# GateLoop attention and a PReLU MLP in one kernel: v's 16-token rows from the input, phases turned by ScalarE, new due times

## The chip, the cores and the metric

The kernel runs on one core of a Trainium2 chip. Time is device time in microseconds (us), lower is better. The engines are TensorE (PE, matmuls; PEld is its weight load), VectorE (DVE), ScalarE (ACT), GpSimd (POOL) and SyncE (SP), which here issues every DMA.

## The reference

Two stages. The first is a linear attention with a complex decay per channel, for 4 batches, 8 heads, 768 tokens and head dimension 48; the second a two-layer MLP on 3072 rows of 384, with 2048 hidden features and a PReLU.

```python
mag = np.sqrt(a_re * a_re + a_im * a_im)
scale = np.minimum(mag, 0.999) / (mag + 1e-06)
a_re_n, a_im_n = (a_re * scale, a_im * scale)
for t in range(S):
    ar, ai = (a_re_n[:, :, t, :, None], a_im_n[:, :, t, :, None])
    new_re = ar * S_re - ai * S_im
    new_im = ar * S_im + ai * S_re
    kv = np.einsum('bhd,bhe->bhde', k[:, :, t], v[:, :, t])
    S_re, S_im = (new_re + kv, new_im)
    y[:, :, t] = np.einsum('bhd,bhde->bhe', q[:, :, t], S_re)
x = y.transpose(0, 2, 1, 3).reshape(B * S, H * D)
h = x @ w_in
g = np.maximum(h, 0.0) + alpha * np.minimum(h, 0.0)
out = g @ w_out
```

## The kernel before

**Units and gates.** Tokens are cut into chunks of 128; a unit is one chunk of one batch, 24 in all. The token loop is replaced by products: a decay is split into a magnitude and a phase (a unit complex number). `gates` runs nine times, each time over one to three chunks of one batch (384, 768 or 1152 values in each of 128 partitions). It computes the magnitudes' products over dyadic blocks (`dec`, stored to the scratch `decs`) and the running product of the phases over tokens (stored to `phs`). Each unit then multiplies q and k with the phases (L678), forms masked products of q and k in blocks of 1, 2, 4, 8, 16 and 32 tokens by `meet` and `mask_out` (L688, L705, L708), where W is ScalarE's copy of one half of k (L753), multiplies these with v's rows (L820), adds what the carried state gives (L827) and stores its result to `ysc` (L847). `loads_x` reads it back as xT (L860), the input of the MLP: `features` (L871, then L879 on ScalarE and L881 on DVE), `outputs` (L891, then L899 and the store L902).

**Phases' layout.** In `gates` the running product over a row of N values is made in L = 8 steps. The values are held as (l n), l outside, so that each step is one contiguous piece; L331 turns them into this order. At the end every block is multiplied with the product of the blocks before it (L440, DVE, 2N values) and the two products are added (L442, DVE, N values). In the kernel before, L442 writes into `ab` in the order of tokens, (n l), a stride of 8 values, and L444 stores `ab` from there to `phs`:

```python
TT(out=p.rearrange("p (n l) -> p l n", l=L), in0=m[:, 0], in1=m[:, 1], op=ALU.add)
used = yield DMA(N / 2, ts)
```

`tmp` has four rows of N: c, d, e and f. d and e are also UT, the operand of both multiplications at L440; c and f hold m, the products.

**v's rows.** For each block size h the product needs v's rows of the even or odd blocks of h tokens, in the tile VL (7 kinds of 2 x 64 partitions). `loads_v` fetches them per unit. For 1, 2, 32 and "odd" they are loaded from the input in pieces at L658: 1 + 1 + 2 + 2 pieces for each of two halves, 12 in all. For the sizes in SPREAD = [4, 8, 16], `half_rows` first copies the rows from the input to a scratch `vsc` in DRAM (L595: 4 DMAs for each size and batch, and for the first chunk alone), and L661 reads the three kinds at once.

**Weights.** w_in and w_out come as pairs of 32-bit words in eight pieces each (L507), through a ring of three buffers in `g_sb`, and are made into f32 by `to_f32` on ScalarE, DVE and TensorE (L520 to L548).

**The order of work.** A planner, `Plan`, writes the order of instructions of each engine ahead of time. Each generator yields its next step with its engine, an estimated cost and what it waits for. Among the steps that can start within 0.1 us of the earliest the planner takes the one that is due first. Due times are written by hand in GATES_DUE, UNIT_DUE and UNIT_STEPS and in the calls of `plan.add` (first, last and number of steps). A cost only shapes the order; the chip then runs each engine's queue in that order and waits where it must. A step of SP is one DMA issue, counted as 0.45 us; `DVE(N)` is 0.17 + 0.00105 N us, `ACT(N)` 0.17 + 0.00085 N us.

Of the kernel before, what the change touches and what calls it, by code (L numbers as in the profile page):

```python
# [11 lines left out]
ALU = mybir.AluOpType  # L12
# [3 lines left out]
P = 128  # L16
# [115 lines left out]
def kernel(  # L132
# [92 lines left out]
    def DVE(n, *after, takes=(), first=False):  # L225
        return "DVE", 0.17 + n * 1.05e-3, after, takes, 0, first

    def ACT(n, *after, takes=(), first=False):
        return "ACT", 0.17 + n * 0.85e-3, after, takes, 0, first
# [7 lines left out]
    def DMA(kb, *after, takes=(), engine="SP"):  # L237
        return engine, 0.45, after, takes, kb, False
# [20 lines left out]
    def gates(b, c0, c1):  # L259
# [57 lines left out]
        L = 8  # L317
# [117 lines left out]


        m = tmp[:, 0::3].rearrange("p a (l n) -> p a l n", l=L)
        for o, p in enumerate((x, y)):
            yield DVE(2 * N, t)
            TT(out=m, in0=UT, in1=turned(off3, o).unsqueeze(2).to_broadcast([P, 2, L, nb]), op=ALU.mult)  # L440
            ts = yield DVE(N)
            TT(out=p.rearrange("p (n l) -> p l n", l=L), in0=m[:, 0], in1=m[:, 1], op=ALU.add)  # L442
            used = yield DMA(N / 2, ts)
            nc.sync.dma_start(phs[o].rearrange("(t p) s -> p t s", p=P), p.rearrange("p (t s) -> p t s", t=NK))  # L444
        t = used
        for u in range(b * NCH + c0, b * NCH + c1):
            done["PP", u] = t
        done["gates", b + last, 0 if last else c1] = used
# [122 lines left out]


    KINDS = ["odd"] + LEVELS
    SPREAD = [4, 8, 16]
    vsc_of = {}

    def half_rows():


        for b, chunks in [(0, 1)] + [(b, NCH) for b in range(B)]:  # L580
            vsc = dram.tile([len(SPREAD), chunks, 2, HC, 2 * D2], F32, tag=f"vsc{chunks}", name="vsc")
            for c in range(1 if (b, chunks) == (0, NCH) else 0, chunks):
                vsc_of[b * NCH + c] = vsc[:, c]
            for i, h in enumerate(SPREAD):
                for n in range(HP):
                    src = v[b, n].rearrange("(m s h) c e -> s m h c e", s=2, h=h)[0]
                    dst = vsc[i, :, n // 2, :, (n % 2) * D2:(n % 2 + 1) * D2].rearrange(
                        "c (m h) e -> m h c e", m=src.shape[0])
                    if chunks == 1:
                        dst, src = dst[:, :, 0], src[:, :, 0]  # L590

                    k = (HP * i + n) * NCH // (HP * len(SPREAD))
                    end = yield DMA(24.5 * chunks, ("KQ", (b - 1) * NCH + k) if b else
                                    ("raw", "in", k // 3 if chunks == 1 else k))
                    nc.sync.dma_start(dst, src)  # L595
            for c in range(1 if (b, chunks) == (0, NCH) else 0, chunks):
                done["halves", b * NCH + c] = end
# [3 lines left out]
    def loads():  # L601
        for u in range(NU):
            b, c = divmod(u, NCH)
            cols = slice(c * P, (c + 1) * P)
            yield DMA(196, takes=(R["KQ"],))
            KQ = work.tile([D2, 2, H, P], F32, tag="KQ", name="KQ", bufs=3)
            for i in range(2):
                rows = slice(i * D, (i + 1) * D)
                if i:
                    yield DMA(196)  # L610
                nc.sync.dma_start(KQ[rows, 0], qv[b, :, :, cols])
                t = yield DMA(196)
                nc.sync.dma_start(KQ[rows, 1], kv_in[b, :, :, cols])
            done["KQ", u] = t
            loaded[u] = L = dict(KQ=KQ)
            for i in range(2):
                rows = slice(i * D, (i + 1) * D)
                t = yield DMA(196, ("PP", u), takes=() if i else (R["PP"],))
                scr, phs, at = scr_of[u]
                if i == 0:  # L620
                    L["PP"] = PP = work.tile([D2, H, P], F32, tag="PP", name="PP", bufs=1)
                nc.sync.dma_start(PP[rows], phs[i].rearrange("(h d) s -> d h s", d=D)[:, :, at * P:(at + 1) * P])
            done["rotation", u] = t
            for i in range(2):
                rows = slice(i * D, (i + 1) * D)
                t = yield DMA(393, ("T", u), takes=() if i else (R["T"],))
                if i == 0:
                    L["T"] = T = work.tile([D2, H, TL], F32, tag="T", name="T", bufs=2)
                nc.sync.dma_start(T[rows], scr.rearrange("(h d) c s -> d h c s", d=D)[:, :, at])
            done["decays", u] = t  # L630

    def loads_v():
        for u in range(NU):
            b, c = divmod(u, NCH)
            yield DMA(196, ("KQ", u), takes=(R["V"],))
            L = loaded[u]
            L["V"] = V = work.tile([P, HP, D2], F32, tag="V", name="V", bufs=2)
            nc.sync.dma_start(V, v[b, :, :, c].rearrange("n p e -> p n e"))
            yield DMA(98)
            VL = work.tile([P, len(KINDS), 2, D2], F32, tag="VL", name="VL", bufs=2)  # L640
            first = True
            for k, h in enumerate(KINDS):
                for i in range(2):
                    tokens = v[b, 2 * i:2 * i + 2, :, c].rearrange("n t e -> t n e")
                    to = VL[HC * i:HC * (i + 1), k]
                    if h in ("odd", 1):
                        runs = [(to, tokens[int(h == "odd")::2])]
                    elif h == 2:
                        runs = [(to[j::2], tokens[j::4]) for j in range(2)]
                    elif h == 32:  # L650
                        runs = [(to[h * m:h * (m + 1)], tokens[2 * h * m:2 * h * m + h]) for m in range(2)]
                    else:
                        runs = []
                    for dst, src in runs:
                        if not first:
                            yield DMA(98 // len(runs))
                        first = False
                        nc.sync.dma_start(dst, src)  # L658
            t = yield DMA(98 * len(SPREAD), ("halves", u))
            k = KINDS.index(SPREAD[0])  # L660
            nc.sync.dma_start(VL[:, k:k + len(SPREAD)].rearrange("p l n e -> p l (n e)"),  # L661
                              vsc_of.pop(u).rearrange("l i t e -> (i t) l e"))
            L["Vp"] = {name: VL[:, i] for i, name in enumerate(KINDS)}
            done["V", u] = t
# [261 lines left out]
    for name in ("own", 2, 4, 8):  # L926
# [2 lines left out]
    done["gates", 0, 0] = (0.0, None)  # L929

    GATES_DUE = [
        (26.3, -358.9), (-328.0, -500.0), (-179.2, -104.7), (231.5, 215.9), (74.2, 238.4),
        (540.5, 303.2), (421.2, 501.6), (664.0, 601.5), (562.3, 925.7)]
    UNIT_DUE = [
        (55.8, 57.9), (20.4, 80.3), (107.9, 169.0), (50.5, 95.0), (275.8, 246.6), (335.9, 313.3),
        (43.9, 199.5), (280.3, 275.6), (311.8, 314.1), (175.3, 359.9), (286.9, 484.9), (523.3, 614.1),
        (483.1, 533.3), (602.0, 688.0), (422.4, 760.9), (498.5, 590.6), (482.1, 685.9), (628.1, 681.9),
        (514.5, 511.7), (850.0, 972.4), (718.0, 832.2), (573.9, 747.6), (1029.2, 947.3), (1075.1, 1018.2)]
    UNIT_STEPS = [
        1.37, 1.44, -1.25, 0.34, 0.06, 0.73, -0.28, 0.17, 0.47, 0.29, 0.10, -1.28,  # L940
        -0.19, 0.89, 0.94, 0.47, -0.37, -0.85, -1.49, -0.06, 0.35, 0.20, -0.85, 0.60,
        1.37, 0.28, -0.19, -0.34, 0.29, -0.08, 0.46, -0.39, 0.38, 0.11, -1.18, 0.44,
        -2.22, -0.49, 1.07, 1.78, 1.02, -0.40, 1.79, 1.28, 0.11, -0.25, -0.85, -1.16,
        0.63, 3.94, 0.80, 2.84, 1.07, 1.11, 1.22, -0.82, -0.14, -1.89]
    with tc.manual_schedule():
        for g, due in zip(GATES, GATES_DUE):
            plan.add(gates(*g), *due, 100)
        plan.add(loads(), 224.1, 956.4, 8 * NU)
        plan.add(half_rows(), 30.3, 1048.1, 4 * (B + 1) * len(SPREAD))
        plan.add(loads_v(), 187.8, 1238.6, 14 * NU)  # L950
        plan.add(pieces(), 49.2, -71.3, 33)
        plan.add(weights("in"), -35.2, 101.3, 11 * 8)
        plan.add(weights("out"), -3.1, 99.9, 11 * 8)
        for u in range(NU):
            plan.add(unit(u), *UNIT_DUE[u], 56, UNIT_STEPS)
        plan.add(loads_x(), -1.0, -1.0, 1)
        plan.add(all_mlp(), 925.1, 925.1, 1)
        plan.run()
# [37 lines left out]
```

## Time and profile before

| | us |
|---|---|
| median of 3 runs (981.25 to 988.17) | 986.29 |
| the profiled execution, its own time | 986.29 |
| its span, first to last instruction | 984.6 |
| TensorE busy / DVE busy / ScalarE busy | 856.2 / 725.5 / 462.9 |
| L442, 18 additions (2254 ns at 1152 values) | 36.4 |
| L331, 18 copies (2335 ns at 1152 values) | 37.5 |
| L658, 288 DMA issues, median of one | 0.598 |
| L595, 60 DMA issues, median of one | 0.676 |

The profile is one execution. Busy time is what an engine spent in instructions; a wait is put down to the instruction or transfer that ended it. Issues of DMAs are not counted as busy, but SP does them one after the other, and their start and duration stand in SP's timeline. The granted clock is TensorE's, as a share of full speed. "<-" reads "from".

### The profile page before, as it was taken

To read this page: it belongs to the slowest core of one execution; us is meant where nothing else is said; L and a number is where in the kernel's file an instruction comes from. 1 tells how busy PE (TensorE), PEld (TensorE's weight loads), DVE (VectorE), ACT (ScalarE), POOL (GpSimd) and SP (SyncE) were. 2 spreads that over 40 slices of the span, in tenths; PEclk is the share of its full clock that TensorE was granted. 3 is DMA by queue.
4 is the path that set the end of the run, shared out by engine and by line. 5 is a ranking of instruction groups with operands and counts; after the bars stand their busy time and mean duration, and the time that the engine had idled before them with its cause. 6 is when DMAs were issued, how large, how long until landed. Compare 5 with 4: busy or idle time off the path is not lost.

```text
span 984.6 us, 24031 instructions
## 1 busy us (share of the span) xinstructions
PE 856.2 (87%) x9984; PEld 625.2 (63%) x9984; DVE 725.5 (74%) x1137; ACT 462.9 (47%) x924; POOL 162.0 (16%) x326
## 2 busy tenths in 40 slices
PE   0735737899897599999899999999999999999998
PEld 0312434678675467677676767777777777777776
DVE  6898897899879478889698778779888666531112
ACT  5554854485458134745283347444754233332122
POOL 3024027000700060006002500060006000000000
PEclk9958866999999589999999999999999999999999
DMA  6955992677268354786757575756566466200000
GB/s 191 202 176 174 242 231 67 165 157 204 73 175 166 119 123 126 157 181 140 178 115 186 99 184 122 165 121 170 119 169 147 105 141 138 67 25 18 17 9 17
DMA packets 190685, 132.44 MB, mean 135 GB/s; under 512 B 67568, under 2 KB 182384, under 8 KB 190576
## 3 DMA queue, kind: packets, MB, share of 16 engines
q1 hardware_dynamic: 190576, 130.90, 55.2%
q8 instruction: 79, 1.29, 0.6%
q14 instruction: 30, 0.25, 0.1%
HBM read 102.54 MB, written 35.68 MB: 140 GB/s over the span
## 4 chain that ended last, share of the span: by engine, by line
PE 67%; DVE 12%; POOL 6%; DMA 4%; SPq 4%; ACT 4%; issue 3%; ACTq 0%; DVEq 0%; POOLq 0%
PE ps_o L891 24%; PE ps_h L871 23%; PE ps_lv L688 7%; PE ps_y L820 4%; PE ps_kv L780 3%; POOL tmp L360 3%; DVE tmp L440 2%; PE ps_lv L728 2%; PE ps_y L827 2%; POOL blk L362 2%; DVE ab L442 2%; DVE tmp L360 2%; PE ps_kt L768 2%; DMA xT<-ysc 1%; DVE tmp L362 1%
## 5 line engine op out<-in xcount | busy, mean ns | idle before, releaser
L871 PE MATMUL ps_h<-xT,w_in_sb 128*128 128x256 f32 (+1 forms) x1344 | 302.7, 357 | 11.9 <-DMA xT<-ysc 10.8
L891 PE MATMUL ps_o<-w_out_sb,g_sb 128*128 128x384 f32 x768 | 302.5, 508 | 5.2 <-DVE g_sb L881 5.1
L871 PEld LDWEIGHTS ps_h<-xT,w_in_sb 128*128 128x128 f32 x1344 | 233.4, 193 | 83.1 <-DMA xT<-ysc 9.7
L879 ACT ACTIVATE g_sb<-ps_h,al 128x256 f32<-128x256 f32 (+1 forms) x224 | 99.3, 443 | 309.4 <-PE ps_h L871 308.4
L881 DVE SCALAR_TENSOR_TENSOR g_sb<-ps_h,al_sm,g_sb 128x256 f32<-128x256 f32 (+1 forms) x224 | 98.8, 442 | 166.9 <-ACT g_sb L879 165.5
L747 DVE TENSOR_TENSOR KQ<-KQ,T 96x512 f32<-96x512 f32 x240 | 167.7, 708 | 50.7 <-PE ps_lv L688 34.5
L891 PEld LDWEIGHTS ps_o<-w_out_sb,g_sb 128*128 128x128 f32 x768 | 133.6, 192 | 58.9 <-DVE g_sb L881 7.8
L688 PE MATMUL ps_lv<-KQ,W 96*64 96x64 f32 x1920 | 84.8, 233 | 36.8 <-ACT W L753 15.1
L688 PEld LDWEIGHTS ps_lv<-KQ,W 96*64 96x64 f32 x1920 | 69.5, 143 | 69.6 <-ACT W L753 35.8
L340 POOL TENSOR_TENSOR decays_sb<-decays_sb 128x72 f32<-128x72 f32 (+5 forms) x24 | 10.8, 448 | 443.5 <-DVE decays_sb L340 442.3
L753 ACT COPY W<-KQ 96x512 f32<-96x512 f32 x120 | 74.4, 624 | 18.0 <-DVE KQ L747 17.5
L678 DVE TENSOR_TENSOR KQ<-KQ,PP 96x2048 f32<-96x2048 f32 x24 | 55.0, 2292 | 3.5 <-DMA PP<-phs 2.7
L360 POOL TENSOR_TENSOR tmp<-blk 128x72 f32<-128x72 f32 (+1 forms) x56 | 33.7, 602 | 124.6 <-ACT blk L391 120.8
L545 PE MATMUL ps_w<-w_in_sb,ident 128*128 128x512 f32 (+1 forms) x32 | 19.7, 707 | 37.0 <-DVE run L402 24.4
L705 ACT ACTIVATE A<-ps_lv,rows 128x64 f32<-128x64 f32 x144 | 37.5, 330 | 17.1 <-PE ps_lv L688 16.5
L360 DVE TENSOR_TENSOR tmp<-tmp 128x576 f32<-128x576 f32 (+2 forms) x63 | 43.4, 690 | 1.8
L820 PE MATMUL ps_y<-A,VL 64*48 64x64 f32 x2304 | 44.2, 219 | 0.0
L546 PE MATMUL ps_w<-g_sb,ident 128*128 128x384 f32 (+2 forms) x64 | 36.0, 651 | 7.9 <-DVE g_sb L538 7.9
L780 PEld LDWEIGHTS ps_kv<-V,KT 64*96 64x96 f32 x704 | 35.8, 167 | 9.7 <-issue 5.7
L440 DVE TENSOR_TENSOR tmp<-tmp,off 128x2304 f32<-128x2304 f32 (+2 forms) x18 | 41.1, 2285 | 1.1 <-ACT off L434 0.8
L842 ACT COPY yT<-ps_y 48x256 f32<-48x256 f32 x96 | 30.8, 366 | 20.4 <-PE ps_y L827 18.6
L820 PEld LDWEIGHTS ps_y<-A,VL 64*48 64x48 f32 x2304 | 38.3, 122 | 2.6 <-issue 2.4
(115 smaller groups left out, 1051.6 us busy)
## 6 DMA issues: line engine op xcount, KB each, us to landing
T<-decs SPq DMA_DIRECT2D x48, 384.0 KB
KQ<-in_q_dram SPq DMA_DIRECT2D x48, 192.0 KB
KQ<-in_k_dram SPq DMA_DIRECT2D x48, 192.0 KB
PP<-phs SPq DMA_DIRECT2D x48, 192.0 KB
decs<-decays_sb SPq DMA_DIRECT2D x7, 1152.0 KB
phs<-ab SPq DMA_DIRECT2D x14, 576.0 KB
vsc<-in_v_dram SPq DMA_DIRECT2D x48, 144.0 KB
VL<-vsc SPq DMA_DIRECT2D x24, 288.0 KB
```

The source lines that it names most:

```text
L360: on(4 * k).tensor_tensor(out=m, in0=w[:, 1::-1].unsqueeze(2).to_broadcast([P, 2, 2, k]), in1=pairs_of(u), op=ALU.mult)
L440: TT(out=m, in0=UT, in1=turned(off3, o).unsqueeze(2).to_broadcast([P, 2, L, nb]), op=ALU.mult)
L678: nc.vector.tensor_tensor(out=KQ, in0=KQ, in1=PP.unsqueeze(1).to_broadcast([D2, 2, H, P]), op=ALU.mult)
L688: nc.tensor.matmul(t[64 * i:64 * i + 64, p], lhsT=weights(4 * i + p), rhs=moving(KQ[:, 0, 4 * i + p]), start=True, stop=True)
L747: nc.vector.tensor_tensor(out=x, in0=x, in1=decays(h)[:, i].unsqueeze(3).to_broadcast([D2, H, n, h]), op=ALU.mult)
L753: nc.scalar.copy(W.rearrange("p n t -> p (n t)").rearrange("p (m h) -> p m h", h=h), halves(KQ[:, 1].rearrange("p n t -> p (n t)"), h)[:, ...
L780: nc.tensor.matmul(kv[s][:, n], lhsT=KT[rows, n], rhs=V[rows, n // 2, (n % 2) * D:(n % 2 + 1) * D], start=True, stop=True)
L820: nc.tensor.matmul(o, lhsT=vp[64 * i:64 * i + 64, s, e_ * D:(e_ + 1) * D], rhs=a[:, HC * own:HC * (own + 1)], start=(name == "own" and not ...
L871: nc.tensor.matmul(p, lhsT=w_in_sb[:, f // 2, kk, f % 2 * P:(f % 2 + 1) * P], rhs=x_of[m][:, kk], start=(kk == 0), stop=(kk == NK - 1))
L879: nc.scalar.activation(gt, p, AF.Relu, scale=al_1[:, f:f + 1])
L881: nc.vector.scalar_tensor_tensor(out=gt, in0=p, scalar=al_sm[:, f:f + 1], in1=gt, op0=ALU.mult, op1=ALU.add)
L891: nc.tensor.matmul(sums[0], lhsT=gt[:, c * P:(c + 1) * P], rhs=w_out_sb[:, f], start=(f == 0), stop=(f == NF - 1))
```

## The change

Three things. In `gates` the last additions write in the order (l n) without stride, and ScalarE copies each of the two results into the order of tokens, from x to d and from y to e, after both additions; the stores read d and e. The next call's wait for `ab` (`used`) is then on the second copy and no longer on the second store. In SPREAD the size 16 is left out: v's rows of 16-token blocks are loaded at L658 in four pieces for each half, 20 pieces a unit in place of 12, and the scratch holds two kinds. All due times of gates, units, their steps and the loads have other values; those of `loads_x` and of the MLP do not. The change is described as loading the first weights piece by piece as well; no line of the diff touches how weights are cut.

```diff
+        tt = []
         for o, p in enumerate((x, y)):
             yield DVE(2 * N, t)
             TT(out=m, in0=UT, in1=turned(off3, o).unsqueeze(2).to_broadcast([P, 2, L, nb]), op=ALU.mult)
-            ts = yield DVE(N)
-            TT(out=p.rearrange("p (n l) -> p l n", l=L), in0=m[:, 0], in1=m[:, 1], op=ALU.add)
-            used = yield DMA(N / 2, ts)
-            nc.sync.dma_start(phs[o].rearrange("(t p) s -> p t s", p=P), p.rearrange("p (t s) -> p t s", t=NK))
-        t = used
+            t = yield DVE(N)
+            TT(out=p.rearrange("p (l n) -> p l n", l=L), in0=m[:, 0], in1=m[:, 1], op=ALU.add)
+            tt.append(t)
+        for o, (p, r) in enumerate(((x, d), (y, e))):
+
+            t = used = yield ACT(2 * N, *tt)
+            nc.scalar.copy(r.rearrange("p (n l) -> p n l", l=L), p.rearrange("p (l n) -> p n l", l=L))
+            t = yield DMA(N / 2, t)
+            nc.sync.dma_start(phs[o].rearrange("(t p) s -> p t s", p=P), r.rearrange("p (t s) -> p t s", t=NK))
...
-    SPREAD = [4, 8, 16]
+    SPREAD = [4, 8]
...
-                    elif h == 32:
-                        runs = [(to[h * m:h * (m + 1)], tokens[2 * h * m:2 * h * m + h]) for m in range(2)]
+                    elif h >= 16:
+                        runs = [(to[h * m:h * (m + 1)], tokens[2 * h * m:2 * h * m + h]) for m in range(HC // h)]
...
     GATES_DUE = [
-        (26.3, -358.9), (-328.0, -500.0), (-179.2, -104.7), (231.5, 215.9), (74.2, 238.4),
-        (540.5, 303.2), (421.2, 501.6), (664.0, 601.5), (562.3, 925.7)]
+        (-251.5, -234.4), (-137.4, -381.1), (-121.1, -13.5), (186.7, 183.0), (96.1, 124.0),
+        (497.4, 308.3), (486.6, 518.2), (594.7, 624.3), (594.1, 831.0)]
...
-        plan.add(loads(), 224.1, 956.4, 8 * NU)
-        plan.add(half_rows(), 30.3, 1048.1, 4 * (B + 1) * len(SPREAD))
-        plan.add(loads_v(), 187.8, 1238.6, 14 * NU)
-        plan.add(pieces(), 49.2, -71.3, 33)
-        plan.add(weights("in"), -35.2, 101.3, 11 * 8)
-        plan.add(weights("out"), -3.1, 99.9, 11 * 8)
+        plan.add(loads(), 54.1, 931.2, 8 * NU)
+        plan.add(half_rows(), 16.8, 1036.5, 4 * (B + 1) * len(SPREAD))
+        plan.add(loads_v(), 236.4, 1199.2, 22 * NU)
+        plan.add(pieces(), -52.1, -100.2, 33)
+        plan.add(weights("in"), -26.9, 98.5, 11 * 8)
+        plan.add(weights("out"), -28.0, 124.3, 11 * 8)
```

## The prediction

> **What bounds the kernel now.** I read the busy times first, then the windows by stage, then the list of waits, the chain, and the order of SP's queue around the longest wait. Busy time and slices (row PE is TensorE's busy tenths):
>
> ```profile
> PE 856.2 (87%) x9984; PEld 625.2 (63%) x9984; DVE 725.5 (74%) x1137; ACT 462.9 (47%) x924; POOL 162.0 (16%) x326
> PE   0735737899897599999899999999999999999998
> DVE  6898897899879478889698778779888666531112
> PEclk9958866999999589999999999999999999999999
> ```
>
> TensorE is full from the fifteenth slice (about 350 us) on. The windows put numbers to it (columns: PE, its weight loads, DVE, ACT, POOL busy; then granted clock, DMA share, GB/s):
>
> ```profile
> 0.00:150.00 150.00, 70.16 (x524) 38.75 (x524) 128.45 (x225) 85.61 (x134) 35.55 (x72) 0.81 0.78 203
> 150.00:350.00 200.00, 166.95 (x2307) 129.74 (x2306) 164.45 (x248) 103.52 (x212) 40.21 (x73) 0.89 0.58 140
> ```
>
> TensorE idles 150 - 70.2 = 79.8 us and 200 - 167.0 = 33.1 us in these two: 112.9 us of the 984.6 - 856.2 = 128.4 us that it idles at all. After 350 us only 15.5 us are left. The matmuls are untouched by the diff, so a change in time must come out of those 112.9 us, or make new gaps. There DVE is 84% busy ((128.5 + 164.5) / 350), ACT 54%. The waits of TensorE before 350 us that matter here:
>
> ```profile
> PE ps_w L545 <- DVE run L402: 24.4, 1, 24.4
> PE ps_lv L688 <- ACT W L753: 15.1, 10, 3.0
> PE ps_h L871 <- DMA xT<-ysc: 9.4, 1, 9.4
> ```
>
> The third is one gap, and SP's queue explains it. SP starts DMAs strictly in order; from 284.0 to 327.5 us it has no pause of 0.2 us:
>
> ```profile
> 290.88 10.70 SPq L658 DMA_DIRECT2D VL<-in_v_dram  x10
> ...
> 316.21 7.06 SPq L658 DMA_DIRECT2D VL<-in_v_dram  x9
> ...
> 325.92 0.54 SPq L860 DMA_DIRECT2D xT<-ysc  x1
> ```
>
> The MLP's input xT stands behind 22 pieces of v. TensorE ran dry at 322.6 and got it at 332.0. The two windows after it show a second price, the clock:
>
> ```profile
> 323.00:332.00 9.00, 0.03 (x1) 0.03 (x1) 2.85 (x5) 0.13 (x1) 0.00 (x0) 0.50 0.79 242
> 332.00:352.00 20.00, 17.66 (x239) 13.84 (x241) 11.50 (x18) 5.84 (x14) 4.99 (x7) 0.67 0.41 92
> ```
>
> At clock 0.67 the 20 us after the gap do about 13.4 us of full-speed work: some 6 us lost on top of 9.4.
>
> **What the Trainium skill says.** "SBUF — State Buffer", section "Door 1: The DMA port swizzle", says that a stride beyond a 16-byte line costs, so 4 fp32 are free. The trace agrees: L442 writes with a stride of 8 fp32 and takes 2254 ns; L313, with the same operation and size and no stride, 1351 ns. "DMA: Bandwidth & Descriptors", section "Anatomy of one DMA", says that a semaphore wait happens on the issuing sequencer before dispatch, not in the DMA engines; SP's "SPq L444 <- DVE ab L442: 56.6, 8, 17.7" agrees. "TensorE: Matmul & The Clock Gate", section "What's actually happening", says that idleness halves the clock; the 0.50 above agrees.
>
> **The parts.**
>
> *Last additions (L442).* Removed: strided writes. 14 x (2254 - 1351) + 2 x (1549 - 951) + 2 x (861 - 559) ns = 14.4 us of DVE; the unstrided rows for 768 and 384 elements are L323 (951) and the minimum of L313 (559). After 350 us TensorE is 98% busy beside it: worth nothing there. Before 350 us lie the calls on 384, 768 and two on 1152 elements: 2 x 0.30 + 2 x 0.60 + 4 x 0.90 = **5.4 us**. They are pieces of the chain of waits there; I take -5, bounds -5.4 and 0.
>
> *ScalarE's copies.* Added: 18, each reading with stride (8 l, n outside). Nearest row is L331, a copy that turns the same layout the other way: 2335, 1635 and 884 ns by size; below, an unstrided ACT pass (L289, 1164 ns). 14 x 2.335 + 2 x 1.635 + 2 x 0.884 = 37.7 us of ACT (half of that below), of which 14.4 before 350 us. ACT has 46% free there, so the sum is hidden; not so what queues behind a 2.3 us copy on an in-order engine: L753 (W, for the next masked product) and L879. At 311.0 and 313.7 us the L331 pair shows it: the next two products waited 2.01 and 0.67 us for W, and one 0.93 us for the product before. So 0 to 3.6 us for a pair. Two large pairs, around 175 and 275 us, fall where TensorE is nearly full: I take +2 each, **+4**, bounds 0 and +11 (the small pairs too). Later pairs: the MLP's matmuls cover them, 0.
>
> *The stores (L444).* Both copies wait for both additions, since they overwrite UT. From the first multiplication the second store was ready after 2 x 2.55 + 2 x 2.25 = 9.6 us, now after 2 x 2.55 + 2 x 1.35 + 2 x 2.34 = 12.5 us, the first after 10.1 instead of 4.8. SP waits in order for them, and x, V and KQ loads queue behind. The consumer of the phases hardly waited (L678 on PP: 2.7 us in all). Two large calls before 350 us at +2.9: 0 to +6, I take **+3**. On the other side ab is free after the copies and no longer after the landing of the stores: SP's wait "L282 <- DMA phs<-ab", 16.5 us in 6 times, goes. It overlaps other lateness; **-2**, bounds -4 and 0.
>
> *v's 16-token rows.* Per unit 8 more pieces at L658 (20 for 12), median 598 ns of SP each: 192 x 0.598 = 114.8 us. Gone: 20 of 60 scratch stores (L595, 676 ns), 13.5 us, and a third of VL<-vsc's bytes, with the same 24 issues. Net +101 us on SP. Bytes: a third of 48 x 144 KB, 12 x 24 KB and 24 x 288 KB, 4.7 MB, go; 192 x 24 KB = 4.6 MB come: nothing. Before 350 us 8 units are loaded: 64 x 0.598 - 14 x 0.676 = +29 us. Where SP has pauses this is hidden. Where it has none it delays what follows: in 284 to 327 us two units' pieces stand before xT, 16 x 0.598 = 9.6, at the 1.07 us seen there up to 17, less one scratch store of 0.7: **+9** for TensorE, bounds 0 and +16, because it already waits. Fourteen xT loads stand in this queue; two already had a wait on them, 9.4 and 1.4 us. I allow for one more late by one unit's pieces: **+5**, bounds 0 and +15 (a gap of the size above with its slow clock).
>
> *First weights piece by piece.* No changed line does this; raw weights come in 16 pieces in both. Zero, apart from the due times.
>
> *Due times.* They reorder every engine's instructions; work stays the same. In the early part loads of units come sooner (54.1 for 224.1), pieces of v later (236.4 for 187.8), gate 0 sooner. Nothing in the trace prices this. Bounds: it may remove the xT gap (-15), or shift the start of the MLP; value 0, as the terms above take the old order.
>
> **Sum:** -5 + 4 + 3 - 2 + 9 + 5 = +14 on the profiled execution's 984.6 us: 998.6, and with the 1.7 us around the span (986.29 - 984.6) **1000 us**. That execution is the median of the three.
>
> **The rivals.**
> A, chance 0.46: SP's queue, the sum above; 992 to 1010.
> B, 0.15, faster: the new order places xT's loads ahead of v's pieces. Place: the gap at 322.6 us. Price: -9.4 - 6 for gap and clock, -5 - 2 + 4 + 3 for the rest, -15.4: 971. It decides if the load leaves SP before about 316 us by the old clock (it took 6.0 us to land). For it: the later due of v's pieces. Against: 8 more of them, and each new order may make another gap.
> C, 0.15, no change: SP's pauses take all additions (it issues during only 19 of the 50 us from 150, and 44 of the 100 us from 750, by its timeline), xT stays as late as it is: -5 + 4 + 3 - 2 = 0, 986.
> D, 0.24, much slower: the early part gets later as a whole. The first xT load leaves SP at 145.8 us, after three units' V; 24 more pieces at the mean 0.73 us are 17 us, and a longer start at half clock costs 6 more: 14 + 23 = +37, 1023. For it: by its timeline SP is busy 45 of the first 50 us and 39 of those from 100 to 150. Against: TensorE did not wait for that first load.
>
> **The numbers.** One per cent, about what a measurement can tell, puts the limits at 976.4 and 996.2. Slower: all of D and 0.38 of A, 0.62. Same: 0.08 of A, C, 0.02 of B, 0.25. Faster: 0.13. Range 970 to 1028: below it half of B, above it a third of D, about 0.15 left out. It holds the summed upper bounds of the terms nearly whole.
>
> **What would show it.** L442 at 1.35 us; 18 new ACT copies at 2.3 us; 480 issues at L658; TensorE's waits on xT above the 10.8 us of now; early idle above 113 us; the late part as full as before. If early idle falls below 100 us and the waits on xT vanish, the reading of SP's queue is wrong; if copies take 1.2 us, ACT's term is.

## The result, and the profile after

The changed kernel takes 1020.27 us (median of 4 runs, 1018.67 to 1024.2) against 985.15 us (4 runs): a ratio of 1.0365, 95% interval 1.0316 to 1.0414. That is 35 us slower. The forecast was 14 us slower, 1000 us; the time lies in the range 970 to 1028, but the change is 2.5 times the forecast one.

The page after, the same rows as before (busy times, TensorE's and DVE's busy tenths, TensorE's clock):

```profile
PE 875.8 (86%) x9984; PEld 638.6 (63%) x9984; DVE 711.2 (70%) x1137; ACT 494.7 (49%) x942; POOL 159.5 (16%) x326
PE   0456746889997899998987999989998989999998
DVE  6798997797869786888668678957778666531112
PEclk9877867898999899999998899999999998999999
```

TensorE's row shows where it went: in the late part several of the 9s have turned into 8s, and one into a 7. The windows of the kernel after, in the stages of the prediction (PE, its weight loads, DVE, ACT, POOL busy; clock, DMA share, GB/s):

```profile
0.00:150.00 150.00, 70.95 (x522) 38.88 (x523) 126.16 (x228) 90.92 (x139) 36.42 (x72) 0.81 0.77 196
150.00:350.00 200.00, 171.99 (x2129) 130.24 (x2128) 159.64 (x242) 105.90 (x200) 42.14 (x83) 0.89 0.55 134
350.00:850.00 500.00, 469.13 (x5931) 348.88 (x5930) 374.06 (x561) 253.13 (x491) 80.97 (x173) 0.97 0.61 137
```

And the third window of the kernel before:

```profile
350.00:850.00 500.00, 488.03 (x6139) 360.38 (x6140) 396.03 (x585) 237.41 (x487) 86.20 (x183) 0.99 0.61 141
```

Up to 350 us TensorE idles 79.1 + 28.0 = 107 us, not more than the 113 us of before. From 350 to 850 us it idles 30.9 us where it idled 12.0, at a mean clock of 0.97 for 0.99. The whole span is 33.3 us longer: 13.7 us more idle, and 19.6 us more busy for the same matmuls, which ran slower. The clock accounts for most of that: the trace's clock records are either 1.0 or 0.5, and summed over them TensorE worked 66 us at 0.5 before and 100 us after. At full clock those 34 us more would have taken 17. The late part, where I had called edits free because TensorE is 98% busy, is where the time was lost.

### The profile page after: what moved, and what is told of

It reads as the page before. It is cut to its first block, busy times and chain, and to the rows that moved or that the text cites. A ratio compares the mean times of both kernels' runs of the same rounds, so it can differ in the third digit from the quotient of the medians.

```text
span 1017.9 us, 24317 instructions
## 1 busy us (share of the span) xinstructions
PE 875.8 (86%) x9984; PEld 638.6 (63%) x9984; DVE 711.2 (70%) x1137; ACT 494.7 (49%) x942; POOL 159.5 (16%) x326
## 4 chain that ended last, share of the span: by engine, by line
PE 56%; DVE 11%; DMA 11%; SPq 8%; POOL 5%; ACT 5%; issue 3%; DVEq 0%; ACTq 0%; POOLq 0%
PE ps_o L896 21%; PE ps_h L876 19%; PE ps_lv L693 5%; SPq L663 5%; PE ps_y L825 4%; PE ps_kv L785 2%; POOL tmp L360 2%; POOL blk L362 2%; PE ps_y L832 2%; DVE tmp L360 2%; DVE tmp L441 2%; DMA VL<-in_v_dram 1%; DMA T<-decs 1%; PE ps_lv L733 1%; DMA KQ<-in_k_dram 1%
## 5 line engine op out<-in xcount | busy, mean ns | idle before, releaser
L876 PE MATMUL ps_h<-xT,w_in_sb 128*128 128x256 f32 (+1 forms) x1344 | 307.9, 362 | 11.0 <-DMA xT<-ysc 11.0
L876 PEld LDWEIGHTS ps_h<-xT,w_in_sb 128*128 128x128 f32 x1344 | 236.0, 196 | 83.7 <-DMA xT<-ysc 12.2
L886 DVE SCALAR_TENSOR_TENSOR g_sb<-ps_h,al_sm,g_sb 128x256 f32<-128x256 f32 (+1 forms) x224 | 99.0, 443 | 181.7 <-ACT g_sb L884 180.0
L693 PE MATMUL ps_lv<-KQ,W 96*64 96x64 f32 x1920 | 86.4, 237 | 34.9 <-ACT W L758 23.4
L683 DVE TENSOR_TENSOR KQ<-KQ,PP 96x2048 f32<-96x2048 f32 x24 | 55.0, 2293 | 14.1 <-issue 6.8
L825 PE MATMUL ps_y<-A,VL 64*48 64x64 f32 x2304 | 49.0, 220 | 0.0
L825 PEld LDWEIGHTS ps_y<-A,VL 64*48 64x48 f32 x2304 | 44.3, 122 | 1.6 <-issue 1.2
L785 PEld LDWEIGHTS ps_kv<-V,KT 64*96 64x96 f32 x704 | 37.9, 176 | 10.3 <-issue 4.8
L785 PE MATMUL ps_kv<-V,KT 64*96 64x48 f32 x704 | 41.0, 262 | 2.6 <-ACT KT L777 2.3
```

The lines of the kernel that those rows point to most:

```text
L683: nc.vector.tensor_tensor(out=KQ, in0=KQ, in1=PP.unsqueeze(1).to_broadcast([D2, 2, H, P]), op=ALU.mult)
L693: nc.tensor.matmul(t[64 * i:64 * i + 64, p], lhsT=weights(4 * i + p), rhs=moving(KQ[:, 0, 4 * i + p]), start=True, stop=True)
L785: nc.tensor.matmul(kv[s][:, n], lhsT=KT[rows, n], rhs=V[rows, n // 2, (n % 2) * D:(n % 2 + 1) * D], start=True, stop=True)
L825: nc.tensor.matmul(o, lhsT=vp[64 * i:64 * i + 64, s, e_ * D:(e_ + 1) * D], rhs=a[:, HC * own:HC * (own + 1)], start=(name == "own" and not ...
L876: nc.tensor.matmul(p, lhsT=w_in_sb[:, f // 2, kk, f % 2 * P:(f % 2 + 1) * P], rhs=x_of[m][:, kk], start=(kk == 0), stop=(kk == NK - 1))
L886: nc.vector.scalar_tensor_tensor(out=gt, in0=p, scalar=al_sm[:, f:f + 1], in1=gt, op0=ALU.mult, op1=ALU.add)
```

## The experiments

Most of them hold the order: the planner counts the same steps, so all engines but SP issue the same work in the same order, and only the instructions under test differ. Then the same matmul can be found by its number in two traces, and the difference of its start shows where time is lost ("by the same matmuls" below). Ratios are to the kernel before, run in the same round, with their 95% intervals. Lines are those of each run's own kernel: L876 and L883 here are L871 of the kernel before, L733 and L740 its L728, L737 and L744 its L732, L683 and L690 its L678.

### Which of the three parts

**The due times alone**, with nothing else of the change:

```diff
-    GATES_DUE = [(26.3, -358.9), (-328.0, -500.0), ...
+    GATES_DUE = [(-251.5, -234.4), (-137.4, -381.1), ...
-        plan.add(loads(), 224.1, 956.4, 8 * NU)
+        plan.add(loads(), 54.1, 931.2, 8 * NU)
...
```

> The kernel before with nothing changed but the due times, which are those of the changed kernel. The order of work alone (theory 1): most of the 35 us come with it, 1010 us or more. v's pieces on SP (theory 2): under 995, as 12 pieces a unit are issued as before. ScalarE's copies (theory 3): under 995 as well.

Measured: 1039.5 us, ratio 1.0553 (1.0511 to 1.0595). The order alone can cost 54 us, more than the whole change.

**The reverse**, the changed kernel with the old due times:

> The changed kernel with the due times of the kernel before. Theory 1: within 10 us of 985. Theories 2 and 3: 1005 or more, since pieces and copies stay. A fourth theory, that due times only fit the very steps they were chosen for: 1005 or more here and in the run with the due times alone.

1043 us, ratio 1.0586 (1.0548 to 1.0624). In this order the kernel does not compute the reference's result, for a reason that was not traced, so its time can carry little; I rest on it only that it is no way back to 985. Each set of due times is bad with the other's steps: the fourth theory fits both runs, theory 1 only the first.

**The changed order without the copies**, additions strided:

```diff
-            TT(out=p.rearrange("p (l n) -> p l n", l=L), in0=m[:, 0], in1=m[:, 1], op=ALU.add)
+            TT(out=p.rearrange("p (n l) -> p l n", l=L), in0=m[:, 0], in1=m[:, 1], op=ALU.add)
...
-            nc.scalar.copy(r.rearrange("p (n l) -> p n l", l=L), p.rearrange("p (l n) -> p n l", l=L))
```

> The changed kernel with every engine's order held, but the last additions write in the order of tokens and ScalarE's 18 copies are not issued; the planner still counts them. Theory 3: falls by 10 us or more from 1020. Theories 1 and 2: stays within 5 us of 1020; my prediction's own terms for this part (-5 +4 +3 -2) say 0.

1035.5 us, ratio 1.0508 (1.0468 to 1.0548). Taking the copies away made it 15 us slower: ScalarE's copies are a gain in this order. Theory 3 falls, and with it my sum of 0 for this part.

**The changed order without the pieces**, 16-token rows through the scratch:

```diff
+    SCR = [4, 8, 16]
...
+                    if n % 2:
+                        copy(2, 2 * i + n // 2)
...
-                        nc.sync.dma_start(dst, src)
+                        if h != 16:
+                            nc.sync.dma_start(dst, src)
```

> The changed kernel with the order of the engines held, but v's 16-token rows go through the scratch again: the 192 pieces are not issued, 20 more scratch stores are, behind the others. Theory 2, which my prediction rests on: falls by 14 us or more from 1020. Theories 1 and 3: stays within 5 us of 1020.

992.0 us (9 runs), ratio 1.0068 (1.0033 to 1.0103). The pieces cost 28 us here.

**Both undone**, so that only the new order is left:

> The changed kernel's order with the instructions of the kernel before: no ScalarE copies, additions in the order of tokens, v's 16-token rows through the scratch. What is left against 985 is the new order alone. If the parts add up (copies gave 15, pieces took 28): 1007. If the copies' gain was only hiding part of the pieces' cost: 992.

1003.0 us, ratio 1.0153 (1.0126 to 1.0179). The four runs in the new order make a square:

```
new order, us        16-token rows by scratch   by pieces
strided additions            1003.0               1035.5
ScalarE's copies              992.0               1020.3
```

Step by step: +16 for the order (1003.0 against 986.6), -11 for the copies, +28 for the pieces. The sum of such steps is the whole difference by itself; what the square shows is that the parts hardly depend on each other. Taken in the other sequence, the pieces are +32 and the copies -15, 4 us away.

### Why the pieces cost

The start of the same matmul in the changed kernel and in after_held_v16:

```
matmul    after   held_v16   later by, us
1660      250.6      250.7     -0.1
3320      398.9      393.8      5.1
4150      466.7      455.7     11.0
5146      568.0      555.4     12.7
7138      731.1      718.8     12.3
7636      769.7      749.6     20.0
9130      893.8      871.3     22.5
```

Nothing up to 250 us, then a few places of 1 to 5 us each. One of them is between 440 and 467 us. SP's timeline of the kernel after (start, duration, issue):

```profile
438.83 0.98 SPq L627 DMA_DIRECT2D PP<-phs  x2
439.93 0.40 SPq L643 DMA_DIRECT2D V<-in_v_dram  x1
440.88 12.17 SPq L663 DMA_DIRECT2D VL<-in_v_dram  x20
453.10 1.13 SPq L666 DMA_DIRECT2D VL<-vsc  x1
454.27 0.70 SPq L600 DMA_DIRECT2D vsc<-in_v_dram  x1
455.08 0.94 SPq L634 DMA_DIRECT2D T<-decs  x2
```

The same place in after_held_v16:

```profile
432.50 8.28 SPq L670 DMA_DIRECT2D VL<-in_v_dram  x12
440.82 0.43 SPq L673 DMA_DIRECT2D VL<-vsc  x1
441.30 1.40 SPq L597 DMA_DIRECT2D vsc<-in_v_dram  x2
442.80 2.90 SPq L640 DMA_DIRECT2D T<-decs  x2
```

T, the decays of the next unit, stands behind 20 pieces instead of 12. From the first piece to T's issue it takes 14.2 us, with 12 pieces 10.3. The chain of waits of the kernel after goes on from there:

```profile
455.55 7.14 DMA T<-decs
...
462.81 0.10 DVE KQ L737
...
463.42 0.47 DVE g_sb L886
...
465.06 0.69 PE ps_lv L693 x16
```

DVE stands at L737 until T has landed, an addition of the MLP (L886) stands behind it in DVE's queue, and TensorE waits for both: 2.5 us at 465 us, none at this matmul in after_held_v16. DVE's waits at L737 in all (after_held_v16 has 6.1 us in their place):

```profile
DVE KQ L737 <- DMA T<-decs: 8.9, 3, 4.7
```

The forecast had named xT as the load that would be late. Against the kernel before, its longest wait stayed (9.4 us, then 9.0). But against the same order without the pieces it grew by 3.9 us; the kernel after, then after_held_v16:

```profile
PE ps_h L876 <- DMA xT<-ysc: 11.0, 2, 9.0
```

```profile
PE ps_h L883 <- DMA xT<-ysc: 7.1, 1, 7.1
```

So xT is late, as forecast, and T is as well. Another kind of gap is this, in TensorE's timeline of the kernel after:

```profile
733.37 1.09 PE L832 MATMUL ps_y<-KQ,St 96*48 96x64 f32 x30
736.79 0.31 PE L832 MATMUL ps_y<-KQ,St 96*48 96x64 f32 x2 [2.32 <-issue]
```

TensorE stops in the middle of 32 equal matmuls, 30 done, and waits for nothing that the profile shows. Summed over TensorE's gaps, those that end with "issue" are 14.8 us after, 6.7 us before, 7.2 us in after_held_v16. Of the 14.8, 3.1 us are waits that this word hides: at 321 and 399 us L733 starts as DVE's L683 ends, which had waited for PP and for T. At the other five stops, and at all that wait for nothing in the traces of before (four) and after_held_v16 (five), TensorE goes on 1.3 to 1.9 us after the end of a 16 KB packet of the DMA queue that the page calls "q8 instruction". That points to TensorE's instructions arriving late. No run tests that by itself.

The two traces can now be set side by side. The profiled executions differ by 24 us (1019.6 and 995.8). TensorE idles 17.5 us longer with the pieces: 3.9 us for xT, 5.0 us behind PP and T (at 321, 399 and 465 us), 5.1 us in the stops without a wait, the rest in small pieces; and it is 5.7 us longer busy. No single load is the cause.

**The pieces in the old order**, issued together behind those of size 2:

```diff
+    SCR = [4, 8]
...
+                    if h == 16:
+                        end = yield DMA(24.5 * chunks, ...)
+                        continue
...
-                        if not first:
+                        if not first and h != 16:
                             yield DMA(98 // len(runs))
```

> The kernel before with the order of all other engines held; v's 16-token rows come in 8 pieces more a unit, issued together behind those of size 2, and the scratch holds two kinds. Theory 2 (pieces cost wherever they stand): 1005 to 1015. If the 28 us were a matter of the new order: under 995. My prediction's terms for it: 999.

1010.2 us, ratio 1.0250 (1.0196 to 1.0303), 24 us more. Here the late load is mainly xT, as forecast; the busy times, the waits of this kernel and SP's timeline ahead of the gap:

```profile
PE 871.1 (86%) x9984; PEld 635.8 (63%) x9984; DVE 724.9 (72%) x1137; ACT 462.7 (46%) x924; POOL 160.0 (16%) x326
PE ps_h L878 <- DMA xT<-ysc: 23.4, 5, 15.5
```

```profile
322.49 2.02 SPq L665 DMA_DIRECT2D VL<-in_v_dram  x3
325.01 1.12 SPq L854 DMA_DIRECT2D ysc<-yT  x2
326.49 9.99 SPq L665 DMA_DIRECT2D VL<-in_v_dram  x17
...
339.03 0.64 SPq L867 DMA_DIRECT2D xT<-ysc  x1
```

From 10.8 us to 23.4 us in waits for xT, and one of 15.5 us. The gaps that end with "issue" did not grow here (5.7 us for 6.7). The waits are half of the price: of the 29.0 us that this execution's span is longer, 13.8 us are idle and 14.9 us are TensorE busy longer with the same matmuls (871.1 for 856.2). Its work at half clock went from 66 to 87 us, which makes 11 of these.

**Issues or bytes:** 192 DMAs that carry almost nothing, on top of after_held_v16:

```diff
+                        else:
+                            nc.sync.dma_start(spare[:, 4 * i + j], src[:, :, 0:1])
```

> after_held_v16 (992 us) with 192 DMAs added at the places of the pieces, each with the same 32 descriptors but one value of 4 bytes in place of a row of 384; nobody reads them. If the pieces cost by SP's issue and the length of the queue: 1010 or more. If they cost by their bytes or by the readers' waits for them: under 998.

1020.9 us, ratio 1.0375 (1.0306 to 1.0445): 29 us for 1/96 of the bytes, with no reader. So the pieces need neither their bytes nor a reader to cost that much. The places are not the same, though: by the same matmuls this run is 5 us behind after_held_v16 at 45 us, where the real pieces had cost nothing, and DVE waits 24.6 us for PP, for 8.7. That both come to 28 or 29 us is in part chance.

**Another issuer:** the 192 pieces from GpSimd.

```diff
-                        nc.sync.dma_start(dst, src)
+                        (nc.gpsimd if h == 16 else nc.sync).dma_start(dst, src)
```

> The changed kernel, but the 192 pieces of 16-token rows are issued by GpSimd at the same places of the order; SP keeps the rest. If the pieces cost because other loads stand behind them in SP's queue: 992 to 1005. If they cost by filling the DMA rings, whoever issues them: 1015 or more. GpSimd's own chain in the gates, behind which the issues may stand, can hide a gain.

1008.7 us, ratio 1.0203 (1.0152 to 1.0254), between the two answers: 12 of the 28 us are gone. TensorE's wait for xT falls from 11.0 to 5.8 us, its gaps that end with "issue" hardly (13.3 for 14.8). SP's queue alone is not shown to be the whole cost; the rest may lie in GpSimd's own queue or in the transfers, whoever issues them.

**Place or number:** all 480 issues stay, those of size 16 go back in the queue.

```diff
+                        if h == 16:
+                            behind.append((dst, src))
+                        else:
+                            nc.sync.dma_start(dst, src)
...
+            flush()
             done["decays", u] = t
```

> The changed kernel, all other engines' order held; all 480 issues stay, but the 8 pieces of a unit's 16-token rows are issued later in SP's queue: behind the next pair of T loads, at the latest ahead of the unit's products that read them; PP and xT loads pass them. If what counts is which load stands behind a piece: 1012 or less. If the number of issues counts: 1015 to 1025. If the pieces then come too late for their readers: above 1025, with TensorE's waits on L825.

1004.5 us, ratio 1.0193 (1.0174 to 1.0213): 16 us less with the same number of issues. The place of the pieces is worth more than half of their cost. But T is not what gained by it. For 21 of the 24 units the pieces were issued at their latest place, ahead of their readers, and T still stands behind all 20; this run at the place shown above:

```profile
434.64 8.37 SPq L674 DMA_DIRECT2D VL<-in_v_dram  x12
...
444.28 4.47 SPq L610 DMA_DIRECT2D VL<-in_v_dram  x8
448.86 0.88 SPq L641 DMA_DIRECT2D T<-decs  x2
```

Of the 24 pairs of T loads three have fewer pieces ahead of them than in the changed kernel, none after 316 us; of the 14 xT loads eleven have, and about half of the stores of the output. DVE's wait for T, 8.9 us in the changed kernel, did not fall:

```profile
DVE KQ L748 <- DMA T<-decs: 12.3, 5, 6.4
```

TensorE's gaps that end with "issue" fall from 14.8 to 5.3 us, its wait for xT stays (10.7 us), and its work at half clock falls from 100 to 80 us. Which of the DMAs that passed the pieces matters is not shown.

### The copies and the order, in the kernel before

**Copies in the old order**, both at the place of the second store:

```diff
+            for i, (src, r) in enumerate(((x, d), (y, e)) if o else ()):
+                nc.scalar.copy(r.rearrange("p (n l) -> p n l", l=L), src.rearrange("p (l n) -> p n l", l=L))
+                nc.sync.dma_start(phs[i].rearrange("(t p) s -> p t s", p=P), r.rearrange("p (t s) -> p t s", t=NK))
```

> The kernel before with every engine's order held, but the additions write without stride and ScalarE copies; both copies and both stores stand at the place of the second store. If this part is worth 15 us whatever the order (dropping it cost the changed kernel 15): 970 to 975. My prediction's terms for it: 985. If it only helps in the order it was planned with: 985 or more.

998.7 us, ratio 1.0125 (1.0073 to 1.0177). The same edit gains 11 to 15 us in one order and loses 12 in the other, where the planner had not counted the copies on ScalarE. By the same matmuls this run is 6 us ahead of the kernel before at 350 us and 9 us behind at the end: the gain that I had forecast for the early part is there, and the loss comes where I had put nothing. DVE's 14 us saved are no gain by themselves.

**A small disturbance** of the due times of the units:

```diff
-        (55.8, 57.9), (20.4, 80.3), ...
+        (53.6, 60.0), (22.0, 78.8), ...
```

> The kernel before with each of the 48 due times of the units moved by up to 3 us at random. If the order is a fitted point and any other order of the planner costs tens of us: 1005 or more. If only the large moves of the due times matter: 980 to 992.

1012.7 us, ratio 1.0272 (1.0224 to 1.0320). Up to 3 us on due times that reach to 1000 cost 26 us. It is one draw, but with the swapped sets it says what other due times can mean: the time of the order before is not shared by any of the other orders here.

### Can SP's queue be made shorter to gain?

Five runs tried it in the kernel before.

```diff
+    MORE = [32]          # the second run: [2, 32]
...
+                    if i >= 3 - len(MORE):
+                        copy(MORE[i - 3], n)
...
+                        if h not in MORE:
+                            nc.sync.dma_start(dst, src)
```

> The kernel before, order of the other engines held, the other way on: v's 32-token rows go through the scratch too. 96 pieces fewer on SP, 20 scratch stores more, 76 issues less. At 28 us for 172 issues, 0.16 us each: 973. If SP was not yet a limit in the kernel before: 985 or more.

1005.5 us, ratio 1.0188 (1.0166 to 1.0210): 76 issues less, and 19 us slower.

> As before_held_scratch32, with the 2-token rows through the scratch as well: 192 pieces fewer, 40 stores more, 152 issues less. At 0.16 us each: 961, less if TensorE has no idle time left to give. If SP was not yet a limit: 985 or more.

987.8 us (15 runs), ratio 1.0006 (0.9983 to 1.0030): 152 issues less, the same time.

The third has the additional scratch stores from the second batch on only (the edit puts "b and" before its condition):

> before_held_scratch2_32 (988), with the additional scratch stores and fewer pieces from the second batch on only, so that nothing is added to SP's queue for the first units. That run lost 14 us by 125 us and won 12 back at the gap before xT. If the early loss came from the first batch's stores: 970 to 978. If from the second batch's, which stand between the first units' loads: 985 or more.

989.4 us (11 runs), ratio 1.0040 (1.0018 to 1.0062). By the same matmuls this run was 16 us behind the kernel before at 305 us, and at 340 us, after the kernel before has waited for xT, 4 us. Its waits from 244 to 262 us:

```profile
PE ps_lv L737 <- issue: 10.7, 1, 10.7
DVE KQ L687 <- DMA PP<-phs: 10.2, 1, 10.2
```

and SP's timeline ahead of them:

```profile
234.96 8.35 SPq L593 DMA_DIRECT2D vsc<-in_v_dram  x4
243.40 4.61 SPq L629 DMA_DIRECT2D PP<-phs  x2
```

The four scratch stores, 2.1 us each, stand before PP, and TensorE waits 10.7 us for the unit that needs it. (Here "issue" hides a wait that the line below it names.) The gap before xT then closes only because TensorE comes there late: xT leaves SP at 332.5 us, in the kernel before at 325.9.

The fourth leaves the scratch as it is and has GpSimd issue the pieces:

```diff
-                        nc.sync.dma_start(dst, src)
+                        (nc.gpsimd if h in (2, 32) else nc.sync).dma_start(dst, src)
```

> The kernel before, with the 8 pieces of a unit for sizes 2 and 32 issued by GpSimd, all at their places in the order. SP's queue loses 192 of 736 issues and nothing is added. If the gap before xT closes and GpSimd's chain does not suffer: 970 to 978. If GpSimd's issues delay the gates: 985 or more.

990.3 us, ratio 1.0044 (1.0027 to 1.0062). The gap before xT is gone here too; the kernel was 12 us behind by then, and xT left SP at 328.2 us.

The fifth is the edit of the moved pieces, for the sizes 2 and 32:

> The kernel before, order of the other engines held, all 288 issues kept; a unit's 8 pieces of sizes 2 and 32 go behind the next pair of T loads, at the latest ahead of their readers. xT in the gap at 332 us then stands behind 16 pieces less. The same edit took 16 us off the changed kernel. If place is the price here too: 972 to 978. If the late loads in the kernel before cost only what other waits would cost as well (scratch2_32 closed the gap and won nothing): 983 to 990.

987.1 us (22 runs), ratio 1.0019 (0.9994 to 1.0045), the same as before. xT had 8 pieces less ahead of it and not 16, and left SP at 327.1 us; its gap is gone because TensorE came there 10 us later. In none of the five runs did this xT leave SP sooner than in the kernel before, so what an earlier xT would be worth is not tested. No run here beats the kernel before.

## Why the prediction was wrong, step by step

**Direction: right.** It was slower, and v's pieces are the largest part of it. That SP's queue carries all of their cost is not shown: only 12 of the 28 us go when GpSimd issues them.

**SP's term, the failed one.** "+9 for TensorE" at the gap before xT and "+5" for one more late load make 14 us; measured were 28 to 32 in the new order and 24 in the old. The step that failed is to price the pieces as TensorE's wait for xT alone. In the old order these waits grew by 12.6 us, so as a sum of waits the term was nearly right. What it left out there is the slower clock around the gaps, which the prediction had itself read as "some 6 us lost on top of 9.4" and then did not put into its +9: TensorE was busy 14.9 us longer. In the new order xT brought 3.9 us of waits; PP and T, which nothing waited for in the profile of before except 2.7 us for PP, brought 5.0 us, and stops without a wait 5.1 us. The upper bounds, 16 + 15, held the 28 us, not the 32.

Two readings in this term were wrong as well. A piece of 16-token rows carries 12 KB, not 24 (VL<-in_v_dram x192, 12.0 KB in the list of issues after), so 2.4 MB of 132.4 went; the term for bytes was zero either way. And SP's issues take 525 us in all after and 466 before, 59 us more and not 101: the median of 598 ns came from pieces of 24 and 48 KB, those of 12 KB have a median of 422 ns in after_pieces_moved_back, where they have a line of their own. SP was given less work than forecast, and TensorE lost twice as much.

**Due times, "value 0".** Measured +16 with the instructions of before, +54 with its steps counted as before. The bounds I gave (-15, or a later start of the MLP) had no room for a loss late in the run, where the 16 us came: at 350 us TensorE has done as much work in after_held_both as in the kernel before. The +16 and the -11 of the next part nearly cancel, by luck; so the total, 35 for 14, looks as if one term were off and hides two more.

**The gates' part, -5 + 4 + 3 - 2 = 0.** Measured -11 to -15 in the new order and +12 in the old. The sizes of the instructions were right:

```profile
L448 ACT COPY tmp<-ab 128x1152 f32<-128x1152 f32 x14 | 30.6, 2182 | 4.0 <-DVE tmp L441 4.0
L443 DVE TENSOR_TENSOR ab<-tmp 128x1152 f32<-128x1152 f32 x14 | 18.9, 1354 | 0.3
```

1354 ns for the 1351 expected, 2182 for 2335, DVE's busy time 14.3 us less for 14.4. What was wrong is "TensorE is 98% busy beside it: worth nothing there". By the same matmuls, after_held_additions was 6.9 us later than the changed kernel at 350 us and 18.3 us at the end: more than half of the loss came where I had put nothing. After 350 us TensorE's waits put down to DVE are 13.6 us in it and 9.3 us in the changed kernel, its gaps that end with "issue" 17.6 and 12.5. So a share of 98% did not mean that DVE had time to spare.

**Against the rivals.** D named about the right time, 1023, by a wrong road: the early part did not get later (107 us idle for 113). B and C are out.

**What was to show it.** 480 issues, L443 and the copies came as said. TensorE's waits on xT hardly grew against the kernel before (11.0 us for 10.8), early idle was below 113 us, and the late part was not as full as before: these three told against the mechanism as I had placed it.

**What stays open.** Why the pieces bring more of TensorE's stops without a wait in the new order and not in the old; which of the DMAs behind the pieces gave the 16 us back when these were moved; and what the 16 us that stay when GpSimd issues the pieces consist of.

## What to carry to other kernels

In a queue that issues in order, price a small DMA by what stands behind it, and not by its bytes: the same 480 issues cost 16 us more or less by their place alone. Look also at loads that nobody waits for yet, and add to each wait the time that TensorE then works at half clock, which accounts for 17 of the 33 us here. An engine at 98% does not make the work of the others free: edits on DVE and ScalarE moved the time by 11 to 15 us, more than half of it in the stage that was 98% full. When an order was searched for, compare edits with the order held, since each new order tried here cost 16 to 54 us. And look in the trace whether an edit moved what it was meant to move: here T stayed behind most of the moved pieces, and the xT that TensorE waited for never left sooner.

## What the runs showed that was not expected

DMAs of 128 bytes in all cost as much as DMAs of 12 KB: 29 us for 192, though not at the same places. A 3 us shake of due times cost 26 us. And a wait of 9.4 us vanished in four runs that were no faster: TensorE had been held up elsewhere by about as much and came there later.
